# Reordering the start, the hand-over and the end of a one-token attention kernel

## The chip, the cores and the metric

The kernel runs on one core of one Trainium2 chip. The metric is the device time of one execution in microseconds. Every kernel below was timed several times, next to runs of the kernel before on the same chip. PE is the matmul engine, PEld its weight loads, DVE the vector engine, ACT the scalar engine, POOL the GpSimd engine and SP the engine that issues most loads. A letter q after an engine's name means its sequencer. A pair of kernels is compared by the ratio of their times, with its 95% interval in brackets.

## The reference

Two attention layers, A and B, each for one new token and 32 heads of size 128. A looks at all 16384 cached keys of a head, B at the last 4096. The two output rows are joined.

```python
# x: (1,1,512); k_cache, v_cache: (1,32,16384,128); wq: (512,4096); wo: (4096,512); all bf16
q = (x @ wq).reshape(1, 1, 32, 128).transpose(0, 2, 1, 3)
k, v = k_cache, v_cache                                # A
k, v = k_cache[:, :, -4096:], v_cache[:, :, -4096:]    # B
p = softmax(einsum("bhqd,bhkd->bhqk", q, k) * 128**-0.5)
o = einsum("bhqk,bhkd->bhqd", p, v)
out = o.transpose(0, 2, 1, 3).reshape(1, 1, 4096) @ wo
```

The caches are nearly all of the traffic: 80 chunks of 2.1 MB for K, 80 for V, and four weight matrices of 4.2 MB; 352 MB in all.

## The kernel before

SP issues the K chunks and ACT the V chunks, into four buffers each. An A head is two chunks, and in B one chunk holds two heads. DVE works on pairs: the two chunks of an A head, or the two heads of a B chunk. Per pair it multiplies K by a replicated q in place, folds 128 products to 8 with four additions, and reduces them to scores. ACT takes the exponentials (and their row sums, `zp`). PE then multiplies them with V (below: PV) into one PSUM bank per head, two banks in turn, and DVE copies each finished sum to `orow`. In the code, `hg` is the head's number (0 to 31 are A's, 32 to 63 B's), z is the sum of a head's exponentials, ot the output row after scaling with 1/z, transposed, and fin its projection with wo.

```python
# SP: loads
sp.dma_start(xrow[0], xs[0]); sp.dma_start(stage, wqs[0]).then_inc(s_wq, 16); sp.dma_start(xrow[1], xs[1])
sp.wait_ge(s_wq, 16)                      # no K load before wq has landed
for ck, c in enumerate(kchunks):
    if ck == NK:                          # B's wq into the same buffer
        sp.wait_ge(s_qmm, 1); sp.dma_start(stage, wqs[1]).then_inc(s_wq, 16)
    if ck >= NK:
        sp.wait_ge(s_hdone, kchunk_maxhead[ck - NK] + 1)     # DVE is done with the buffer
    sp.dma_start(kbuf[ck % NK], kchunk_src(c)).then_inc(s_kdma[ck % NK], 16)
# ACT: waits for s_wq as well, then V chunks in the same way, as PV frees the buffers
# ... cut ...
# DVE, after each pair:
def head_hooks(hg):
    if hg == 1: qB_copies(0)
    if hg == 3: qB_copies(1)
    if hg - 2 >= 0: orow_copy(hg - 2)     # waits for PV of head hg - 2
    if hg == NHEAD + 1: tail_z(0)         # waits for PE's z matmul: sum of zp, then 1/z
    if hg == NHEAD + 3: tail_ot(0)
# PE, after PV of head hg:
    if hg == NHEAD: tail_pe_z(0); tail_pe_ot(0)     # z; 32 matmuls: orow * (1/z), transposed
    if hg == NHEAD + 4: tail_pe_fin(0)              # 32 matmuls of 512 columns: A's projection
# after head 63: the same for B, one after the other
tail_pe_z(1); tail_pe_ot(1); tail_pe_fin(1)
```

The softmax here doesn't subtract the row's maximum and nothing guards it: scores larger than these inputs give would overflow.

## Time and profile before

The median was 872.11 us (870.71 to 874.21, 4 runs); the profiled execution spans 870.8 us.

| what | value |
|---|---|
| DMA traffic | 353 MB, near 428 GB/s in most of the span |
| DVE busy | 771.6 us, 89% |
| PE busy | 420.7 us, 48% |
| last DVE reduction ends | 850.74 us |
| from there to the end | 20.06 us |

From the page of the kernel before: the busy line (engine, us, share of the span, number of instructions), and the rate of the DMA queues in 40 slices of 21.8 us each.

```profile
PE 420.7 (48%) x5322; PEld 389.5 (45%) x5324; DVE 771.6 (89%) x673; ACT 24.2 (3%) x129; POOL 3.9 (0%) x8
...
GB/s 330 431 426 391 419 415 416 418 426 427 427 427 427 428 423 428 429 427 426 427 425 419 427 428 427 427 427 419 400 428 424 421 420 417 404 404 421 421 294 1
```

The queues are full or nearly so (391 to 431 GB/s, with the DMA engines busy for 90% or more of each slice) from the second slice to the 38th. The next listing, the stretch table of the kernel before, shows where they are not. Its columns are: stretch, its length, busy time and instruction count of PE, PEld, DVE, ACT and POOL, the granted PE clock, DMA share and GB/s.

```profile
12.00:13.00 1.00, 0.00 (x0) 0.00 (x0) 0.00 (x0) 0.00 (x0) 0.00 (x0) 1.00 0.61 255
13.00:14.00 1.00, 0.60 (x4) 0.34 (x4) 0.13 (x1) 0.00 (x0) 0.00 (x0) 1.00 0.00 0
14.00:15.00 1.00, 0.19 (x1) 0.13 (x2) 0.76 (x4) 0.00 (x0) 0.00 (x0) 1.00 0.84 213
...
72.00:74.00 2.00, 2.00 (x21) 1.16 (x19) 2.00 (x5) 0.00 (x0) 0.00 (x0) 1.00 0.77 328
74.00:76.00 2.00, 2.00 (x40) 2.00 (x37) 2.00 (x4) 0.00 (x0) 0.00 (x0) 1.00 0.67 147
```

There is a hole at 12 to 15 us, when wq has landed and nothing else has been issued yet, and a shallower one at 73 to 77 us.

The next listing is the timeline of DVE in the kernel before, around the change from A to B. Its columns are: start, duration, engine, line, operation, result and operands, count, and in brackets the idle time before it and what ended it. L440 is the multiplication that opens a pair.

```profile
665.50 8.76 DVE L440 TENSOR_TENSOR kbuf<-kbuf,qbc 128x8192 bf16<-128x8192 bf16 x2 [0.71 <-DMA kbuf<-in_A_k_cache_dram]
...
684.11 4.47 DVE L440 TENSOR_TENSOR kbuf<-kbuf,qbc 128x4096 bf16<-128x4096 bf16 x2
...
697.19 0.18 DVE L365 COPY zsb<-psum 1x32 f32<-1x32 f32 x1 [3.01 <-PE psum L569]
...
697.96 4.49 DVE L440 TENSOR_TENSOR kbuf<-kbuf,qbc 128x4096 bf16<-128x4096 bf16 x2
...
730.90 0.28 DVE L357 CAST orow<-psum 1x128 bf16<-1x128 f32 x1 [2.98 <-PE psum L623]
731.11 4.47 DVE L440 TENSOR_TENSOR kbuf<-kbuf,qbc 128x4096 bf16<-128x4096 bf16 x2
...
741.11 4.47 DVE L440 TENSOR_TENSOR kbuf<-kbuf,qbc 128x4096 bf16<-128x4096 bf16 x2
```

The last wait for a K load is the one of 0.71 us at 665 us. After 731 us the pairs follow each other at exactly 10.0 us. Between 684 and 731 us two steps are longer, 13.85 and 13.05 us: at 697 DVE had waited 3.01 us for PE's z matmul, and at 731 it had waited 2.98 us for a PV that stood behind the 32 projection matmuls.

The end, from the timeline of the kernel before:

```profile
850.02 0.72 DVE L458 TENSOR_REDUCE s<-kbuf 128x32 bf16<-128x256 bf16 x2
...
851.05 5.95 PE L623 MATMUL psum<-vbuf,e 128*1 128x128 bf16 x64 [4.64 <-ACT e L309]
...
858.05 0.95 PE L581 MATMUL psum<-invz_b,orow 1*128 1x1 bf16 x32 [0.99 <-DVE invz_b L373]
...
859.28 8.67 PE L595 MATMUL psum<-stage,ot_bf 128*1 128x512 bf16 x32 [0.28 <-DVE ot_bf L379]
...
868.00 1.21 DVE L507 CAST out_sb<-psum 1x1024 bf16<-1x1024 f32 x1 [8.77 <-PE psum L595]
```

This is all serial: last reduction, PV of heads 62 and 63, z and 1/z, 32 small matmuls, 32 projection matmuls (8.67 us), copy of the output row, store.

### The profile page before, as it was taken

How to read it: one execution, taken by the hardware profiler on the slowest of the kernel's cores; microseconds unless marked ns; L12 is line 12 of the kernel's file. 1: busy time of each engine (PE TensorE's matmuls, PEld its weight loads, DVE VectorE, ACT ScalarE, POOL GpSimd, SP SyncE). 2: the span in 40 equal slices, each digit the busy share in tenths (PEclk: the TensorE clock that was granted, in tenths of full speed). 3: DMA queues.
4: the chain of work that ended last, by engine and by line, in shares of the span. 5: the costliest groups of instructions: out<-in, count | busy, mean ns of one | idle time of the engine just before them, and what ended most of it. 6: DMA issues, size and time to landing. Idle time of an engine off the chain costs nothing.

```text
span 870.8 us, 11997 instructions
## 1 busy us (share of the span) xinstructions
PE 420.7 (48%) x5322; PEld 389.5 (45%) x5324; DVE 771.6 (89%) x673; ACT 24.2 (3%) x129; POOL 3.9 (0%) x8
## 2 busy tenths in 40 slices
PE   3109644434444444554544444453565447665557
PEld 1006544334444444544544344453565445655544
DVE  0599968798998999999899989988999898999992
ACT  0000000000000000000000000000000000000000
POOL 0000000000000000000000000000000000000000
PEclk9658865667777667677777767676678778678877
DMA  8999999999999999999999999999999999999970
GB/s 330 431 426 391 419 415 416 418 426 427 427 427 427 428 423 428 429 427 426 427 425 419 427 428 427 427 427 419 400 428 424 421 420 417 404 404 421 421 294 1
DMA packets 30330, 353.11 MB, mean 406 GB/s; under 512 B 2627, under 2 KB 2629, under 8 KB 4678
## 3 DMA queue, kind: packets, MB, share of 16 engines
q1 hardware_dynamic: 14630, 176.17, 48.4%
q10 hardware_dynamic: 13568, 167.78, 45.7%
q0 software_dynamic: 2080, 8.39, 2.4%
q8 instruction: 42, 0.69, 0.3%
q14 instruction: 10, 0.08, 0.0%
HBM read 352.32 MB, written 0.00 MB: 405 GB/s over the span
## 4 chain that ended last, share of the span: by engine, by line
DVE 61%; DMA 32%; PE 5%; issue 1%; SPq 1%; DVEq 0%; ACT 0%; ACTq 0%
DMA kbuf<-in_A_k_cache_dram 31%; DVE kbuf L440 28%; DVE kbuf L447 28%; DVE s L458 3%; PE psum L623 3%; PE psum L595 2%; DMA stage<-in_A_wq_dram 1%; DVE orow L357 1%; SPq L274 1%; DVE qbc L341 0%; DVEq L434 0%; DVE out_sb L507 0%; PE psum L581 0%; ACT e L309 0%; ACTq L290 0%
## 5 line engine op out<-in xcount | busy, mean ns | idle before, releaser
L623 PE MATMUL psum<-vbuf,e 128*1 128x128 bf16 x5120 | 382.9, 251 | 389.9 <-ACT e L309 347.3
L623 PEld LDWEIGHTS psum<-vbuf,e 128*1 128x1 bf16 x5120 | 374.0, 99 | 399.3 <-ACT e L309 388.6
L440 DVE TENSOR_TENSOR kbuf<-kbuf,qbc 128x8192 bf16<-128x8192 bf16 (+1 forms) x96 | 351.7, 3702 | 53.6 <-DMA kbuf<-in_A_k_cache_dram 53.5
L447 DVE TENSOR_TENSOR kbuf<-kbuf 128x1024 bf16<-128x1024 bf16 (+4 forms) x384 | 350.0, 980 | 0.0
L458 DVE TENSOR_REDUCE s<-kbuf 128x64 bf16<-128x512 bf16 (+1 forms) x96 | 52.3, 585 | 0.0
L309 ACT ACTIVATE e<-s 128x128 bf16<-128x128 bf16 (+1 forms) x64 | 17.2, 269 | 811.2 <-DVE s L458 771.1
L542 PE MATMUL psum<-stage,xrep 128*128 128x512 bf16 x23 | 7.7, 505 | 41.4 <-DMA stage<-in_B_wq_dram 41.2
L357 DVE CAST orow<-psum 1x128 bf16<-1x128 f32 x64 | 16.1, 269 | 8.6 <-PE psum L623 8.6
L542 PEld LDWEIGHTS psum<-stage,xrep 128*128 128x128 bf16 x24 | 2.9, 125 | 46.2 <-issue 45.1
L595 PE MATMUL psum<-stage,ot_bf 128*1 128x512 bf16 x64 | 16.4, 420 | 0.3 <-DVE ot_bf L379 0.3
L330 DVE CAST xrep<-psum 128x128 bf16<-128x128 f32 x8 | 1.8, 284 | 13.0 <-PE psum L518 13.0
L334 DVE CAST qbc<-psum 128x512 bf16<-128x512 f32 x8 | 4.9, 683 | 9.5 <-PE psum L530 9.5
L309 ACT ACTIVATION_READ_ACCUMULATOR e<-s 128x1 f32 x64 | 11.9, 186 | 0.0
L595 PEld LDWEIGHTS psum<-stage,ot_bf 128*1 128x1 bf16 x64 | 5.8, 92 | 10.1 <-issue 3.2
L530 PE MATMUL psum<-stage,xrep 128*128 128x512 bf16 x32 | 9.4, 465 | 1.0 <-DVE xrep L330 1.0
L507 DVE CAST out_sb<-psum 1x1024 bf16<-1x1024 f32 x1 | 1.2, 1212 | 8.8 <-PE psum L595 8.8
L518 PE MATMUL psum<-ones_row,xrow 1*128 1x128 bf16 x8 | 1.2, 299 | 12.6 <-DMA xrow<-in_B_x_dram 10.5
L530 PEld LDWEIGHTS psum<-stage,xrep 128*128 128x128 bf16 x32 | 3.6, 115 | 6.5 <-issue 3.0
L518 PEld LDWEIGHTS psum<-ones_row,xrow 1*128 1x128 bf16 x8 | 0.7, 124 | 12.9 <-DMA xrow<-in_B_x_dram 10.8
L244 POOL DMA_DIRECT2D stage<-in_B_wo_dram x1 | 1.7, 1682 | 636.2 <-PE psum L595 636.2
L341 DVE CAST qbc<-psum 128x512 bf16<-128x512 f32 x6 | 3.7, 685 | 0.0
L365 DVE COPY zsb<-psum 1x32 f32<-1x32 f32 x2 | 0.3, 174 | 3.0 <-PE psum L569 3.0
(18 smaller groups left out, 13.1 us busy)
## 6 DMA issues: line engine op xcount, KB each, us to landing
kbuf<-in_A_k_cache_dram SPq DMA_DIRECT2D x64, 2048.0 KB, 16.6
vbuf<-in_A_v_cache_dram ACTq DMA_DIRECT2D x64, 2048.0 KB, 17.6
kbuf<-in_B_k_cache_dram SPq DMA_DIRECT2D x16, 2048.0 KB, 23.9
vbuf<-in_B_v_cache_dram ACTq DMA_DIRECT2D x16, 2048.0 KB, 29.8
stage<-in_A_wq_dram SPq DMA_DIRECT2D x1, 4096.0 KB, 12.2
stage<-in_B_wq_dram SPq DMA_DIRECT2D x1, 4096.0 KB, 41.0
stage<-in_A_wo_dram POOLq DMA_DIRECT2D x1, 4096.0 KB, 88.6
stage<-in_B_wo_dram POOLq DMA_DIRECT2D x1, 4096.0 KB, 56.5
```

The costliest lines, as they stand in the source:

```text
L274: sp.dma_start(chunk_dst(kbuf[b], c), kchunk_src(c)).then_inc(s_kdma[b], 16)
L309: act.activation(out=ebuf[b][:, :n_t], in_=sbuf_s[b][:, :n_t], func=mybir.ActivationFunctionType.Exp, scale=SM_SCALE, accum_out=zp[:, hg : ...
L334: ins = dve.tensor_copy(out=qbc[0][:, n * 512 : (n + 1) * 512], in_=bank(n))
L341: ins = dve.tensor_copy(out=qbc[1][:, n * 512 : (n + 1) * 512], in_=bank(2 + n))
L357: dve.tensor_copy(out=orow[0:1, (hg % NHEAD) * DH : (hg % NHEAD + 1) * DH], in_=o_acc(hg % 2),).then_inc(s_orow, 1)
L440: ins = dve.tensor_tensor(out=jb.kview3, in0=jb.kview3, in1=jb.qb, op=mybir.AluOpType.mult)
L447: ins = dve.tensor_tensor(out=jb.kview3[:, :, 0:w], in0=jb.kview3[:, :, 0:w], in1=jb.kview3[:, :, w : 2 * w], op=mybir.AluOpType.add,)
L458: ins = dve.tensor_reduce(out=sbuf_s[jb.b][:, jb.col0 : jb.col0 + jb.rpp], in_=jb.kview3[:, :, 0:RED_W], axis=mybir.AxisListType.X, op=myb ...
L530: ins = pe.matmul(out=bank(n), lhsT=xrep[0][:, c, :], rhs=stage[:, c, n * 512 : (n + 1) * 512], start=(c == 0), stop=(c == 3),)
L542: ins = pe.matmul(out=bank(2 + n), lhsT=xrep[1][:, c, :], rhs=stage[:, c, n * 512 : (n + 1) * 512], start=(c == 0), stop=(c == 3),)
L595: ins4 = pe.matmul(out=psum[0:1, FINBANK * BANK + X * NOUT : FINBANK * BANK + (X + 1) * NOUT], lhsT=ot_bf[:, X * NHEAD + t : X * NHEAD + t ...
L623: last_ins = pe.matmul(out=o_acc(b), lhsT=ebuf[hg % NSE][:, col : col + 1], rhs=vbuf[vb][:, (j0 + j) * DH : (j0 + j + 1) * DH], start=(tdo ...
```

## The change

The intent is (1) to start DVE and the K loads sooner, by loading 512 columns of A's wq first and moving everything that B's q needs to later; (2) to take DVE's waits out of the change from A to B; (3) to do z, the scaling and the projection of B's first 24 heads before the end. The core of the diff, shortened:

```diff
# start, SP
+sp.dma_start(xrow[1], xs[1])
-sp.dma_start(stage, wqs[0]).then_inc(s_wq, 16)
+sp.dma_start(stage[:, :, :512], wqs[0][:, :512]).then_inc(s_wq1, 16)
-sp.wait_ge(s_wq, 16)
 for ck, c in enumerate(kchunks):
+    if ck == 2: sp.dma_start(stage[:, :, 512:], wqs[0][:, 512:]).then_inc(s_wq, 16)
# start, DVE: only q of heads 0..3 is copied first; after head 1:
 if hg == 1:
+    qA_rest_copies(); x_rep_copies(1)
     qB_copies(0)
# start, PE
+x_rep_mms(1) and B's q only after qA_rest_copies
# middle, DVE
-if hg == NHEAD + 1: tail_z(0)
+if hg == NHEAD + 2: tail_z(0)            # one pair later, ahead of orow_copy
# middle, PE
-if hg == NHEAD: tail_pe_z(0); tail_pe_ot(0)
-if hg == NHEAD + 4: tail_pe_fin(0)
+if hg == NHEAD: tail_pe_z(0)
+if hg == NHEAD + 1: tail_pe_ot(0)
+if NHEAD + 4 <= hg < NHEAD + 8: tail_pe_fin(0, (hg - NHEAD - 4) * 8, 8)
# end: B in two segments, heads 32..55 and 56..63
+SEGS = [(0, NHEAD), (NHEAD, NHEAD - 8), (2 * NHEAD - 8, 8)]
+DVE: if hg == 58: tail_z(1);  if hg == 60: tail_ot(1)
+PE:  if hg == 57: tail_pe_z(1);  if hg == 59: tail_pe_ot(1);  if hg == 61: tail_pe_fin(1)
-tail_pe_z(1); tail_pe_ot(1); tail_pe_fin(1)       # 32 heads
+tail_pe_z(2); tail_pe_ot(2); tail_pe_fin(2)       # 8 heads
```

More of the change, by code (lines that the diff above doesn't have):

```diff
@@ L135, in bass_concat_heads__gqa_block_cached__sliding_block_cached__decode_kernel @@
         orow = ctx.enter_context(nc.sbuf_tensor("orow", [1, NHEAD * DH], BF16))
-        zsb = ctx.enter_context(nc.sbuf_tensor("zsb", [1, NHEAD], FP32))
-        invz_f = ctx.enter_context(nc.sbuf_tensor("invz_f", [1, NHEAD], FP32))
-        invz_b = ctx.enter_context(nc.sbuf_tensor("invz_b", [1, NHEAD], BF16))
+        zsb = ctx.enter_context(nc.sbuf_tensor("zsb", [1, 2 * NHEAD], FP32))
+        invz_f = ctx.enter_context(nc.sbuf_tensor("invz_f", [1, 2 * NHEAD], FP32))
+        invz_b = ctx.enter_context(nc.sbuf_tensor("invz_b", [1, 2 * NHEAD], BF16))
         ot_bf = ctx.enter_context(nc.sbuf_tensor("ot_bf", [P, 2 * NHEAD], BF16))
@@ L156, in bass_concat_heads__gqa_block_cached__sliding_block_cached__decode_kernel @@
         s_x = [sem("s_xA"), sem("s_xB")]
+        s_wq1 = sem("s_wq1")
         s_wq = sem("s_wq")
@@ L233, in woA @@
                 def woA():
-                    pool.wait_ge(s_qmm, 3)
+                    pool.wait_ge(s_qmm, 4)
                     pool.dma_start(
@@ L254, in _ @@
                 sp.dma_start(xrow[0][0:1, :], xs[0][0, 0:1, :]).then_inc(s_x[0], 16)
+                sp.dma_start(xrow[1][0:1, :], xs[1][0, 0:1, :]).then_inc(s_x[1], 16)
                 sp.dma_start(
-                    stage_wq_view(), wqs[0][:, :].rearrange("(c p) n -> p c n", p=P)
-                ).then_inc(s_wq, 16)
-                sp.dma_start(xrow[1][0:1, :], xs[1][0, 0:1, :]).then_inc(s_x[1], 16)
+                    stage_wq_view()[:, :, :512],
+                    wqs[0][:, :512].rearrange("(c p) n -> p c n", p=P),
+                ).then_inc(s_wq1, 16)
                 wq_b_issued = False
-                sp.wait_ge(s_wq, 16)
                 for ck, c in enumerate(kchunks):
@@ L263, in _ @@
                     r = ck // NK
+                    if ck == 2:
+                        sp.dma_start(
+                            stage_wq_view()[:, :, 512:],
+                            wqs[0][:, 512:].rearrange("(c p) n -> p c n", p=P),
+                        ).then_inc(s_wq, 16)
                     if ck == NK and not wq_b_issued:
-                        sp.wait_ge(s_qmm, 1)
+                        sp.wait_ge(s_qmm, 2)
                         sp.wait_ge(s_wq, 16)
@@ L325, in dv_inc, with x_rep_copies @@
                     return dv[0]
-                for X in range(2):
+                def x_rep_copies(X):
                     dve.wait_ge(s_xmm, X + 1)
@@ L331, in _, with qA_rest_copies @@
                     ins.then_inc(s_xrep, 1)
+                x_rep_copies(0)
                 dve.wait_ge(s_qmm, 1)
-                for n in range(8):
-                    ins = dve.tensor_copy(out=qbc[0][:, n * 512 : (n + 1) * 512], in_=bank(n))
-                ins.then_inc(s_qcopy, 1)
+                dve.tensor_copy(out=qbc[0][:, 0:512], in_=bank(0)).then_inc(s_qcopy, 1)
+                def qA_rest_copies():
+                    dve.wait_ge(s_qmm, 2)
+                    for n in range(1, 8):
+                        ins = dve.tensor_copy(
+                            out=qbc[0][:, n * 512 : (n + 1) * 512], in_=bank(n)
+                        )
+                    ins.then_inc(s_qcopy, 1)
                 def qB_copies(phase):
                     if phase == 0:
-                        dve.wait_ge(s_qmm, 2)
+                        dve.wait_ge(s_qmm, 3)
                         for n in range(6):
@@ L345, in qB_copies @@
                     else:
-                        dve.wait_ge(s_qmm, 3)
+                        dve.wait_ge(s_qmm, 4)
                         for n in range(6, 8):
@@ L360, in orow_copy, with tail_z @@
                     ).then_inc(s_orow, 1)
-                def tail_z(X):
-                    dve.wait_ge(s_z, X + 1)
+                SEGS = [(0, NHEAD), (NHEAD, NHEAD - 8), (2 * NHEAD - 8, 8)]
+                def tail_z(si):
+                    h0, nh = SEGS[si]
+                    dve.wait_ge(s_z, si + 1)
                     dv_inc(
                         dve.tensor_copy(
-                            out=zsb[0:1, :],
-                            in_=psum[0:1, ZBANK * BANK : ZBANK * BANK + NHEAD],
+                            out=zsb[0:1, h0 : h0 + nh],
+                            in_=psum[0:1, ZBANK * BANK + h0 : ZBANK * BANK + h0 + nh],
                         )
@@ L370, in tail_z, with tail_ot @@
                     dve.wait_ge(s_dv, dv[0])
-                    dv_inc(dve.reciprocal(out=invz_f[0:1, :], in_=zsb[0:1, :]))
+                    dv_inc(dve.reciprocal(out=invz_f[0:1, h0 : h0 + nh], in_=zsb[0:1, h0 : h0 + nh]))
                     dve.wait_ge(s_dv, dv[0])
-                    dve.tensor_copy(out=invz_b[0:1, :], in_=invz_f[0:1, :]).then_inc(
-                        s_zr, 1
-                    )
-                def tail_ot(X):
-                    dve.wait_ge(s_ot, X + 1)
-                    dve.tensor_copy(
-                        out=ot_bf[:, X * NHEAD : (X + 1) * NHEAD],
-                        in_=psum[0:P, OTBANK * BANK : OTBANK * BANK + NHEAD],
+                    dve.tensor_copy(
+                        out=invz_b[0:1, h0 : h0 + nh], in_=invz_f[0:1, h0 : h0 + nh]
+                    ).then_inc(s_zr, 1)
+                def tail_ot(si):
+                    h0, nh = SEGS[si]
+                    dve.wait_ge(s_ot, si + 1)
+                    dve.tensor_copy(
+                        out=ot_bf[:, h0 : h0 + nh],
+                        in_=psum[0:P, OTBANK * BANK + h0 : OTBANK * BANK + h0 + nh],
                     ).then_inc(s_otc, 1)
@@ L429, in job_pre @@
                         dve.wait_ge(s_qcopy, 1)
+                    if hg == 4 and jb.first_of_head:
+                        dve.wait_ge(s_qcopy, 2)
                     if hg == NHEAD and jb.first_of_head:
-                        dve.wait_ge(s_qcopy, 3)
+                        dve.wait_ge(s_qcopy, 4)
                     if hg >= NSE and jb.first_of_head:
@@ L476, in head_hooks @@
                     if hg == 1:
+                        qA_rest_copies()
+                        x_rep_copies(1)
                         qB_copies(0)
@@ L479, in head_hooks @@
                         qB_copies(1)
+                    if hg == NHEAD + 2:
+                        tail_z(0)
                     if hg - 2 >= 0:
                         orow_copy(hg - 2)
-                    if hg == NHEAD + 1:
-                        tail_z(0)
                     if hg == NHEAD + 3:
                         tail_ot(0)
+                    if hg == 2 * NHEAD - 6:
+                        tail_z(1)
+                    if hg == 2 * NHEAD - 4:
+                        tail_ot(1)
                 i = 0
@@ L503, in _ @@
                     orow_copy(hg)
-                tail_z(1)
-                tail_ot(1)
+                tail_z(2)
+                tail_ot(2)
                 dve.wait_ge(s_fin, 2)
@@ L514, in _, with x_rep_mms @@
                 pe.wait_ge(s_ones, 1)
-                for X in range(2):
+                def x_rep_mms(X):
                     pe.wait_ge(s_x[X], 16)
                     for c in range(4):
-                        ins = pe.matmul(
+                        insx = pe.matmul(
                             out=bank(X * 4 + c, 0, P),
@@ L524, in _ @@
                         )
-                    ins.then_inc(s_xmm, 1)
-                pe.wait_ge(s_xrep, 2)
-                pe.wait_ge(s_wq, 16)
+                    insx.then_inc(s_xmm, 1)
+                x_rep_mms(0)
+                pe.wait_ge(s_xrep, 1)
                 for n in range(8):
+                    if n == 0:
+                        pe.wait_ge(s_wq1, 16)
+                    elif n == 1:
+                        pe.wait_ge(s_wq, 16)
                     for c in range(4):
@@ L536, in _ @@
                         )
+                    if n == 0:
+                        ins.then_inc(s_qmm, 1)
                 ins.then_inc(s_qmm, 1)
-                pe.wait_ge(s_qcopy, 1)
+                pe.wait_ge(s_qcopy, 2)
+                x_rep_mms(1)
+                pe.wait_ge(s_xrep, 2)
                 pe.wait_ge(s_wq, 32)
@@ L551, in qB_pass2 @@
                 def qB_pass2():
-                    pe.wait_ge(s_qcopy, 2)
+                    pe.wait_ge(s_qcopy, 3)
                     for n in range(6, 8):
@@ L562, in qB_pass2, with tail_pe_z @@
                     ins2.then_inc(s_qmm, 1)
-                def tail_pe_z(X):
-                    pe.wait_ge(s_exp, NHEAD * (X + 1))
-                    pe.wait_ge(s_qcopy, 3)
-                    if X == 1:
-                        pe.wait_ge(s_otc, 1)
+                SEGS = [(0, NHEAD), (NHEAD, NHEAD - 8), (2 * NHEAD - 8, 8)]
+                def tail_pe_z(si):
+                    h0, nh = SEGS[si]
+                    pe.wait_ge(s_exp, h0 + nh)
+                    pe.wait_ge(s_qcopy, 4)
                     pe.matmul(
-                        out=psum[0:1, ZBANK * BANK : ZBANK * BANK + NHEAD],
+                        out=psum[0:1, ZBANK * BANK + h0 : ZBANK * BANK + h0 + nh],
                         lhsT=ones_col[:, 0:1],
-                        rhs=zp[:, X * NHEAD : (X + 1) * NHEAD],
+                        rhs=zp[:, h0 : h0 + nh],
                         start=True,
@@ L575, in tail_pe_z, with tail_pe_ot @@
                     ).then_inc(s_z, 1)
-                def tail_pe_ot(X):
-                    pe.wait_ge(s_zr, X + 1)
-                    pe.wait_ge(s_orow, NHEAD * (X + 1))
-                    for t in range(NHEAD):
+                def tail_pe_ot(si):
+                    h0, nh = SEGS[si]
+                    pe.wait_ge(s_zr, si + 1)
+                    pe.wait_ge(s_orow, h0 + nh)
+                    for hg in range(h0, h0 + nh):
                         ins3 = pe.matmul(
-                            out=psum[0:P, OTBANK * BANK + t : OTBANK * BANK + t + 1],
-                            lhsT=orow[0:1, t * DH : (t + 1) * DH],
-                            rhs=invz_b[0:1, t : t + 1],
+                            out=psum[0:P, OTBANK * BANK + hg : OTBANK * BANK + hg + 1],
+                            lhsT=orow[0:1, (hg % NHEAD) * DH : (hg % NHEAD + 1) * DH],
+                            rhs=invz_b[0:1, hg : hg + 1],
                             start=True,
@@ L588, in tail_pe_ot, with tail_pe_fin @@
                     ins3.then_inc(s_ot, 1)
-                def tail_pe_fin(X):
-                    pe.wait_ge(s_otc, X + 1)
+                def tail_pe_fin(si, a=0, n=None):
+                    h0, nh = SEGS[si]
+                    X = 0 if h0 < NHEAD else 1
+                    h0, nh = h0 + a, nh if n is None else n
+                    pe.wait_ge(s_otc, si + 1)
                     pe.wait_ge(s_wo, 16 * (X + 1))
                     wo_view = stage_wo_view()
-                    for t in range(NHEAD):
+                    for hg in range(h0, h0 + nh):
+                        h = hg % NHEAD
                         ins4 = pe.matmul(
                             out=psum[0:1, FINBANK * BANK + X * NOUT : FINBANK * BANK + (X + 1) * NOUT],
-                            lhsT=ot_bf[:, X * NHEAD + t : X * NHEAD + t + 1],
-                            rhs=wo_view[:, t, :],
-                            start=(t == 0),
-                            stop=(t == NHEAD - 1),
-                        )
-                    ins4.then_inc(s_fin, 1)
+                            lhsT=ot_bf[:, hg : hg + 1],
+                            rhs=wo_view[:, h, :],
+                            start=(h == 0),
+                            stop=(h == NHEAD - 1),
+                        )
+                    if h0 + nh == NHEAD or h0 + nh == 2 * NHEAD:
+                        ins4.then_inc(s_fin, 1)
                 for hd in heads:
@@ L635, in _ @@
                         tail_pe_z(0)
+                    if hg == NHEAD + 1:
                         tail_pe_ot(0)
-                    if hg == NHEAD + 4:
-                        tail_pe_fin(0)
-                tail_pe_z(1)
-                tail_pe_ot(1)
-                tail_pe_fin(1)
+                    if NHEAD + 4 <= hg < NHEAD + 8:
+                        tail_pe_fin(0, (hg - NHEAD - 4) * 8, 8)
+                    if hg == 2 * NHEAD - 7:
+                        tail_pe_z(1)
+                    if hg == 2 * NHEAD - 5:
+                        tail_pe_ot(1)
+                    if hg == 2 * NHEAD - 3:
+                        tail_pe_fin(1)
+                tail_pe_z(2)
+                tail_pe_ot(2)
+                tail_pe_fin(2)
 _INS = ['A_x', 'A_k_cache', 'A_v_cache', 'A_wq', 'A_wo', 'B_x', 'B_k_cache', 'B_v_cache', 'B_wq', 'B_wo']
```

## The prediction

Two sentences that no trace of this case shows are cut from it where marked. No term of its sum was in them: it is 872.1 - 1.5 - 8.5 = 862 us, as recorded. The two clocks behind its rates can be read in the kernel before: 32 PV matmuls took 1.95 us (61 ns each) at 698.9 us, with a granted clock of 1.00, and the first projections of the end took 0.43 us each from 859.3 to 862.6 us, with a granted clock of 0.50.

> **What bounds the kernel now.** The DMA queues. The stretch table shows 409 to 432 GB/s, a DMA share near 1.0, in nearly every stretch from 16 us to 840 us; 352 MB at about 428 GB/s are 823 of the 870.8 us. [...] DVE, busy 89%, is second: the wait view has it idle 53.5 us for K loads. So work taken off DVE or PE in the middle only lengthens those waits. Time can be won only (a) where the DMA queues are dry and (b) after the last K load.
>
> **(a) Dry queues.** Near 13 us, because K and V are issued only after wq has landed: the stretches between 12 and 18 us lack 2.9 us of traffic. Near 74 us 1.9 us are lacking.
> **(b) The tail.** The traffic stops at 844 us; the last DVE pair runs 841.1 to 850.75. From there 20.05 us are serial: 64 PV matmuls 5.97, z to ot_bf 2.3, 32 projection matmuls 8.7 (0.43 us each for the first 8, then 0.21), copy and store 2.8.
>
> **The start.** wq is cut: 512 columns, then K0 and K1, then the rest. DVE's first multiply moves from 35.8 us to about 14 (estimate: 0.5 + 4.2 MB at 428 GB/s after 2.8 us). I expect nearly all of these 21 us to be lost again: the second head needs K2 and K3, which now share the DMA with V (landing near 42 us, estimate), and after it DVE must copy the rest of qA, rebuild x for B and wait for 24 qB matmuls. Its third head should start near 78 us, as before (77.4). The dry spot at 13 us goes (-2.9 us). The one near 74 us does not: PV of head 0 waits for copies that DVE makes only after its second head, so V buffers come free only near 82 us, when K6 and K7 are about in; 2 to 3.5 us dry. Net: traffic ends 1 to 2 us earlier, K79 with it.
>
> **The middle.** Moving z by one pair and spreading the 32 A projection matmuls over four heads removes DVE stalls of 3.0 and 3.0 us (697, 731 us). DMA was at full rate there: worth about 0.
>
> **The tail.** z, ot and the projection of heads 32 to 55 move ahead, into PE's idle time (53% busy there). The end keeps 8 ot and 8 projection matmuls: 8.7 us become 1.7 to 3.4, ot 0.95 becomes 0.25. The 24 early ones (5 to 6 us) stand directly before the last PV and may delay it by 0.5 us, but leave PE warm: 64 PV matmuls at 61 ns (rate seen at 698 us) are 3.9 instead of 5.97 us. [...] Together 20.05 becomes about 12.
>
> **Sum.** 872.1 - 1.5 - 8.5 = 862 us, range 856 to 867. Faster by over 2% (below 854.7): 0.08; within 2%: 0.91; slower: 0.01.
>
> **What would show it.** First multiply near 14 us but third head near 78; middle rate unchanged, traffic ending near 842; last DVE reduction near 849; then about 12 us.
>
> **What would make it wrong.** A longer dry spot near 80 us; the early B projection delaying the last PV by more than 1 us; or K running ahead of V once DVE stalls less, so that the last V load, not DVE, starts the tail.

## The result, and the profile after

The changed kernel took 858.44 us (median of 11 runs, 856.94 to 860.95), the kernel before 873.1 us (median of its 16 runs by then, 870.68 to 878.45). The ratio is 0.9835, with a 95% interval of 0.9818 to 0.9852. Ratios compare the runs of the two kernels in the same rounds, so they are not quite the ratio of the medians. A gain "by ratio" below is one minus that ratio, times the median of the kernel before in those rounds: here 14.4 us. The range and the class (within 2%) were met.

From the page of the changed kernel, the busy line:

```profile
PE 416.0 (49%) x5324; PEld 384.7 (45%) x5326; DVE 772.5 (90%) x677; ACT 24.1 (3%) x129; POOL 3.9 (0%) x8
```

DVE is busy for 772.5 us, as before: its idle time shrank, its work did not. The stretch table of the changed kernel, where the holes were or were expected:

```profile
12.00:13.00 1.00, 0.00 (x0) 0.00 (x0) 0.00 (x0) 0.00 (x0) 0.00 (x0) 1.00 1.11 475
13.00:14.00 1.00, 0.00 (x0) 0.00 (x0) 0.00 (x0) 0.00 (x0) 0.00 (x0) 1.00 0.74 318
...
80.00:82.00 2.00, 1.34 (x25) 1.34 (x26) 2.00 (x2) 0.40 (x2) 0.00 (x0) 1.00 0.95 401
82.00:84.00 2.00, 2.00 (x39) 2.00 (x37) 2.00 (x1) 0.00 (x0) 0.00 (x0) 1.00 0.95 401
```

The hole at 12 to 15 us is gone, to a dent of 318 GB/s in one microsecond. So is the one at 73 to 77 us: the rate is 393 or more from 72 to 76 us, and 401 or more from there to 90 us.

DVE's timeline of the changed kernel, the same part as before (L460 is now the multiplication):

```profile
681.58 4.47 DVE L460 TENSOR_TENSOR kbuf<-kbuf,qbc 128x4096 bf16<-128x4096 bf16 x2
...
692.15 4.47 DVE L460 TENSOR_TENSOR kbuf<-kbuf,qbc 128x4096 bf16<-128x4096 bf16 x2
...
703.67 0.48 DVE L371 CAST orow<-psum 1x128 bf16<-1x128 f32 x2 [1.17 <-PE psum L619]
...
704.17 4.47 DVE L460 TENSOR_TENSOR kbuf<-kbuf,qbc 128x4096 bf16<-128x4096 bf16 x2
...
784.16 4.47 DVE L460 TENSOR_TENSOR kbuf<-kbuf,qbc 128x4096 bf16<-128x4096 bf16 x2
...
794.87 0.28 DVE L371 CAST orow<-psum 1x128 bf16<-1x128 f32 x1 [0.84 <-PE psum L666]
795.08 4.47 DVE L460 TENSOR_TENSOR kbuf<-kbuf,qbc 128x4096 bf16<-128x4096 bf16 x2
```

B starts 2.5 us earlier, and the steps of 13 us are gone. The two longest steps that are left both have a wait for PE in them: 12.02 us, with 1.17 us for the small matmuls (L619) and the z arithmetic, and 10.92 us, where a sum was copied 0.84 us late because its PV was late. The wait view of the changed kernel (waiter, releaser, us in total, times, longest) gives a reason that the kernel before does not have in its list:

```profile
PE psum L666 <- DMA vbuf<-in_B_v_cache_dram: 30.7, 7, 7.2
```

The end, from the timeline of the changed kernel:

```profile
840.11 5.34 PE L637 MATMUL psum<-stage,ot_bf 128*1 128x512 bf16 x24
...
845.14 0.72 DVE L478 TENSOR_REDUCE s<-kbuf 128x32 bf16<-128x256 bf16 x2
...
846.16 3.73 PE L666 MATMUL psum<-vbuf,e 128*1 128x128 bf16 x64 [0.71 <-ACT e L315]
...
851.37 1.89 PE L637 MATMUL psum<-stage,ot_bf 128*1 128x512 bf16 x8 [0.26 <-DVE ot_bf L397]
853.29 1.21 DVE L533 CAST out_sb<-psum 1x1024 bf16<-1x1024 f32 x1 [1.98 <-PE psum L637]
```

From the last reduction (845.86 us) to the end of the span 10.24 us are left of 20.06. The 24 early projections end at 845.45 us, 0.7 us before the last PV. That PV takes 3.73 instead of 5.95 us, the last projection 1.89 instead of 8.67.

In the two profiles the 14.7 us divide into 2.5 (B starts earlier), 2.4 (from B's start to the last reduction) and 9.8 (from there to the end). The experiments ask what part of the change made each, and why.

### The profile page after: what moved, and what is told of

Same layout as the page of the kernel before. It is cut to its first block, busy times and chain, and to the rows that moved or that the text cites. A ratio compares the mean times of both kernels' runs of the same rounds, so it can differ in the third digit from the quotient of the medians.

```text
span 856.1 us, 12014 instructions
## 1 busy us (share of the span) xinstructions
PE 416.0 (49%) x5324; PEld 384.7 (45%) x5326; DVE 772.5 (90%) x677; ACT 24.1 (3%) x129; POOL 3.9 (0%) x8
## 4 chain that ended last, share of the span: by engine, by line
DVE 49%; DMA 44%; PE 5%; issue 1%; SPq 1%; DVEq 0%; ACT 0%
DMA kbuf<-in_A_k_cache_dram 35%; DVE kbuf L460 22%; DVE kbuf L467 22%; DMA vbuf<-in_B_v_cache_dram 8%; PE psum L666 4%; DVE s L478 3%; PE psum L578 1%; SPq L280 1%; DVE qbc L346 0%; DVE qbc L355 0%; DVE orow L371 0%; PE psum L619 0%; PE psum L637 0%; DVE out_sb L533 0%; DVEq L454 0%
## 5 line engine op out<-in xcount | busy, mean ns | idle before, releaser
L666 PE MATMUL psum<-vbuf,e 128*1 128x128 bf16 x5120 | 378.1, 249 | 378.4 <-ACT e L315 329.8
L666 PEld LDWEIGHTS psum<-vbuf,e 128*1 128x1 bf16 x5120 | 369.2, 98 | 388.7 <-ACT e L315 346.6
L460 DVE TENSOR_TENSOR kbuf<-kbuf,qbc 128x8192 bf16<-128x8192 bf16 (+1 forms) x96 | 351.7, 3703 | 58.2 <-DMA kbuf<-in_A_k_cache_dram 57.2
L619 PE MATMUL psum<-invz_b,orow 1*128 1x1 bf16 x64 | 2.1, 160 | 6.3 <-DVE invz_b L390 6.3
L619 PEld LDWEIGHTS psum<-invz_b,orow 1*128 1x128 bf16 x64 | 1.9, 95 | 6.7 <-DVE invz_b L390 6.6
## 6 DMA issues: line engine op xcount, KB each, us to landing
vbuf<-in_B_v_cache_dram ACTq DMA_DIRECT2D x16, 2048.0 KB, 31.1
```

What stands on the lines that cost most here:

```text
L460: ins = dve.tensor_tensor(out=jb.kview3, in0=jb.kview3, in1=jb.qb, op=mybir.AluOpType.mult)
L619: ins3 = pe.matmul(out=psum[0:P, OTBANK * BANK + hg : OTBANK * BANK + hg + 1], lhsT=orow[0:1, (hg % NHEAD) * DH : (hg % NHEAD + 1) * DH], ...
L666: last_ins = pe.matmul(out=o_acc(b), lhsT=ebuf[hg % NSE][:, col : col + 1], rhs=vbuf[vb][:, (j0 + j) * DH : (j0 + j + 1) * DH], start=(tdo ...
```

## The experiments

Two readings compete. The one of the prediction: DMA bounds everything up to the end, so time is won only where its queues ran dry, and after the last load. The rival: from about 684 us on DVE waits for no K load, so DVE bounds the B heads, and the stalls taken out of the middle are real time.

### One part of the change at a time

Each of the three kernels is the kernel before with one group of the hunks above; the other two groups are left as they were. All three ran on one chip, next to the same runs of the kernel before (median 872.78 us).

`start_only`:

```diff
+the hunks marked "start" (split wq, K0 and K1 ahead of its rest, B's q later)
 tail_z, tail_pe_ot and tail_pe_fin as in the kernel before
```

> Only the new order of the start; the tail and the middle as in the kernel before. Theory (time is won where the DMA queues were dry, and at the tail): last DVE reduction and end both 2 to 4 us earlier than in the kernel before, ratio 0.995 to 0.998. Rival (the 21 us by which DVE starts earlier are worth something in themselves): more than 5 us earlier. Rival 2 (DVE stalls in the middle gave all of the 4.9 us by which the last reduction came earlier): 0 us, ratio 1.000.

Measured: 870.71 us, ratio 0.9966 (0.9942 to 0.9989), or 3.0 us by ratio. The first multiplication was at the same 15 us as in the changed kernel, 21 us earlier than in the kernel before, B's first one at 681.29 us instead of 684.11, and the last reduction at 848.66 us instead of 850.74. Of 21 us, 3 reached the end.

`middle_only`:

```diff
-if hg == NHEAD + 1: tail_z(0)
+if hg == NHEAD + 2: tail_z(0)
-if hg == NHEAD: tail_pe_z(0); tail_pe_ot(0)
+if hg == NHEAD: tail_pe_z(0)
+if hg == NHEAD + 1: tail_pe_ot(0)
-if hg == NHEAD + 4: tail_pe_fin(0)
+if NHEAD + 4 <= hg < NHEAD + 8: tail_pe_fin(0, (hg - NHEAD - 4) * 8, 8)
 start and end as in the kernel before
```

> Only the middle of the change: z of the first 32 heads one pair later on DVE, their projection spread over four heads; start and end as in the kernel before. Theory as predicted (DMA was at full rate there): 0 to 1 us, ratio 0.999 to 1.001. Rival (from about 684 us on DVE waits for no K load in either trace, so DVE is the bound there and its stalls of 6 us, less the new ones of 2 us, are real time): 2 to 4 us earlier, ratio 0.995 to 0.998.

Measured: 871.1 us, ratio 0.9971 (0.9945 to 0.9997), or 2.5 us by ratio: the rival's number, though the upper end of the interval still touches the prediction's 0 to 1 us. The trace and `before_no_woB` below decide. DVE's timeline of this kernel, two pairs at the change from A to B and two near the end:

```profile
695.10 4.47 DVE L444 TENSOR_TENSOR kbuf<-kbuf,qbc 128x4096 bf16<-128x4096 bf16 x2
...
707.13 4.47 DVE L444 TENSOR_TENSOR kbuf<-kbuf,qbc 128x4096 bf16<-128x4096 bf16 x2
...
817.89 4.47 DVE L444 TENSOR_TENSOR kbuf<-kbuf,qbc 128x4096 bf16<-128x4096 bf16 x2
...
828.28 4.49 DVE L444 TENSOR_TENSOR kbuf<-kbuf,qbc 128x4096 bf16<-128x4096 bf16 x2 [0.25 <-issue]
```

From its first B multiplication to its last reduction it takes 162.9 us; the kernel before takes 166.6. The steps of 13.85 and 13.05 us have become 12.03 and 10.0. Steps above 10.0 turn up later, as the 10.39 us before 828.28, and the wait view of this kernel has PV waiting for B's V loads seven times, 31.1 us in all.

`tail_only`:

```diff
+SEGS = [(0, NHEAD), (NHEAD, NHEAD - 8), (2 * NHEAD - 8, 8)], with z, ot and projection of
+heads 32..55 after heads 57, 59 and 61
 start and middle as in the kernel before
```

> Only the early z, ot and projection of heads 32 to 55; start and middle as in the kernel before. Theory: from the last DVE reduction to the end 10 to 10.5 us instead of 20, and the reduction itself within 1 us of the kernel before (it gets about 1 us of z work on DVE earlier), so 9 to 10 us in all, ratio 0.988 to 0.990. Rival: the end moves by less, 6 to 7 us, because the 24 early projections only come cheap when the rest of the change is there.

Measured: 865.16 us, ratio 0.9897 (0.9873 to 0.9921), or 9.0 us by ratio. From the last reduction to the end it took 10.63 us in the profile. The reduction itself came 1.9 us later than in the kernel before's profile, where 1 us was expected at most. 1.1 us of that was there already at B's first multiplication (685.18), before this kernel differs in anything that runs, and some 0.7 us are the z work and the copy of `ot_bf` that now stand between DVE's last pairs.

The three parts add up: 3.0 + 2.5 + 9.0 = 14.5 us, against 14.4 of the whole. As each is uncertain by about 2 us, so close a match is in part luck.

### What the start is worth, and why

`no_gap` is the kernel before without one line:

```diff
 wq_b_issued = False
-sp.wait_ge(s_wq, 16)
 for ck, c in enumerate(kchunks):
```

> The kernel before with one line less: the K queue no longer waits for wq before it issues the first four K loads, so these stand right behind wq in the same queue. wq is not split and V still waits for wq. Theory (the start is worth what the dry spot near 13 us cost): the first B multiply near 681 instead of 684 us and the end 2 to 3 us earlier, ratio 0.996 to 0.998, as in the run with the new start alone (0.9966). Rival (the split of wq and the DVE start at 15 us are what pays): 0 to 1 us, ratio 0.999 or more.

Measured: 870.28 us, ratio 0.9957 (0.994 to 0.9974), or 3.8 us by ratio. As far as the intervals tell, the removed line is worth as much as the whole new start (3.0 us, on another chip). DVE's timeline of this kernel, the multiplications (L439) of the first and third head:

```profile
29.77 8.76 DVE L439 TENSOR_TENSOR kbuf<-kbuf,qbc 128x8192 bf16<-128x8192 bf16 x2
...
74.43 8.75 DVE L439 TENSOR_TENSOR kbuf<-kbuf,qbc 128x8192 bf16<-128x8192 bf16 x2
```

DVE starts at 29.77 us, far later than with the new start (14.88), and its third head at 74.43 us is still the earlier one (75.70 in the changed kernel, 77.35 before). So the early start of DVE at 15 us is not what paid. The first multiplication comes 6.0 us sooner than in the kernel before (35.80), with the K loads right behind wq. The hole near 74 us goes too: `simple` (below), which has the same start, moved 414 GB/s or more in every stretch of 2 us from 72 to 84 us, where the kernel before fell to 147. B's first multiplication came at 680.4 to 682.1 us in eight of the nine profiles of kernels with the new or the one-line start and four buffers each for K and V (the ninth, 686.5 us, is of the kernel `no_woB` below and fell on its slowest run), and at 684.1 to 685.2 us in the four with the old start.

`simple` puts that one-line start under the middle and the end of the change:

```diff
 start of the kernel before
-sp.wait_ge(s_wq, 16)
 middle and end of the changed kernel
```

> Middle and tail of the change, but the start of the kernel before with only the K queue's wait for wq removed (wq whole, DVE starts near 30 us instead of 15). Theory (of the start only the filled dry spot near 13 us counts, not the early DVE): 0.982 to 0.985 of the kernel before, within 1.5 us of the changed kernel. Rival (the early DVE start adds to it once the tail is shorter): 2 us or more slower than the changed kernel, 0.986 or more.

`after_again` is the changed kernel itself, beside it on the same chip:

```diff
 (the changed kernel, no edit)
```

> The changed kernel itself once more, as the measure for the two runs beside it on the same chip. Every theory: 0.9835 of the kernel before, within the interval of 0.982 to 0.985.

Measured: `after_again` 859.67 us, ratio 0.9837 (0.9819 to 0.9856); `simple` 858.14 us, ratio 0.9828 (0.9813 to 0.9843). The split of wq, its extra semaphore and the moved q copies can be left out, at no loss that the runs show.

### What bounds the B heads

Both kernels were run without the 4.2 MB load of B's wo, which falls into the B heads. Their B output is wrong, as A's wo is used twice.

```diff
 woA()
-woB()
-pe.wait_ge(s_wo, 16 * (X + 1))
+pe.wait_ge(s_wo, 16)
```

> The kernel before without the 4.2 MB load of B's wo; the second half of the output is wrong on purpose (A's wo is used in its place). If DMA bounds the B heads, as the prediction had it, some 9.8 us less traffic bring the end 5 to 9.8 us earlier, ratio 0.989 to 0.994. If DVE bounds them from 684 us on (16 pairs at a pitch of 10.0 us and 7 us of stalls, no K wait), the end moves by less than 1 us, ratio 0.999 to 1.001, while the traffic ends earlier.

> The same taken away from the changed kernel, wrong on purpose in the same way. If with the shorter stalls DMA has become the bound there (PV waits for V seven times, 31 us in all, and hold DVE up by some 2 us), the last DVE reduction comes about 2 us earlier and the end with it: about 0.981 of the kernel before. If DMA bounds the B heads fully: 5 us or more, 0.978 or less. If DVE alone: no change, 0.9835.

`before_no_woB`: 873.35 us, ratio 0.9994 (0.9976 to 1.0013). No gain shows: by the interval it is 2.1 us at most, where 5 to 9.8 us were expected of a kernel bound by DMA. Its stretch table and DVE timeline:

```profile
832.00:834.00 2.00, 2.00 (x22) 2.00 (x20) 2.00 (x2) 0.00 (x0) 0.00 (x0) 0.50 0.01 4
```

```profile
841.23 4.47 DVE L439 TENSOR_TENSOR kbuf<-kbuf,qbc 128x4096 bf16<-128x4096 bf16 x2
```

The traffic was over by 832 us, where that of the kernel before lasted to 844, and the last DVE pair still started at 841.23 us (841.07 before). In the B heads of the kernel before, DVE with its two stalls for PE was the bound, not DMA.

`no_woB`, the same taken from the changed kernel: 857.49 us, ratio 0.9811 (0.979 to 0.9832), where the changed kernel had 0.9835 and 0.9837. That is about 2 us, as expected of a kernel in which DMA has become a part of the bound, but the intervals overlap, so the size is not shown. Its profile fell on its slowest run (861.61 us), so its absolute times are left out. From the first B multiplication to the last reduction it takes 162.4 us, against 164.3 and 165.5 in the changed kernel's two profiles, and its wait view has no PV that waits for V. But `simple` and `better`, with the load of wo, come to 163.2 and 162.7 us.

`four_acc` attacks the waits for a late PV from DVE's side: four PSUM banks for the PV sums, so that DVE copies a sum four heads later and need not wait for a late PV.

```diff
-def o_acc(b): return psum[0:1, b * BANK : b * BANK + DH]
+def o_acc(b): b = (0, 1, 6, 7)[b]; return psum[0:1, b * BANK : b * BANK + DH]
-if hg - 2 >= 0: orow_copy(hg - 2)
+if hg - 4 >= 0: orow_copy(hg - 4)        # A's tail_ot and tail_pe_ot two heads later
-if hg >= 2: pe.wait_ge(s_orow, hg - 1)
+if hg >= 4: pe.wait_ge(s_orow, hg - 3)
```

> The changed kernel with four PSUM banks for the PV sums instead of two, so DVE copies a head's sum four heads later and does not wait for a PV that waits for V. Theory (the 4.3 us by which the 16 B pairs exceed 160 us are such waits): first B multiply to last reduction 161 to 162 us instead of 164.3 unless K loads become the wait, the end 1.5 to 3 us earlier than the changed kernel, 0.980 to 0.982 of the kernel before. Rival (DMA sets the pace and K waits replace these waits): no change, 0.9835.

Measured: 859.06 us (4 runs), ratio 0.9832 (0.9805 to 0.9858): no gain that shows, and 165.3 us for the B heads instead of the 161 to 162 expected, as the rival had it. DVE's timeline of this kernel, two pairs in a row:

```profile
786.05 4.49 DVE L461 TENSOR_TENSOR kbuf<-kbuf,qbc 128x4096 bf16<-128x4096 bf16 x2 [3.04 <-DMA kbuf<-in_B_k_cache_dram]
...
796.95 4.49 DVE L461 TENSOR_TENSOR kbuf<-kbuf,qbc 128x4096 bf16<-128x4096 bf16 x2 [0.81 <-DMA kbuf<-in_B_k_cache_dram]
```

DVE's waits for PE are gone from the B heads, and it waits 3.04 and 0.81 us for K loads. It is not shown that the one came in place of the other, for `after_again`, the changed kernel with its two banks, has such a wait too:

```profile
785.55 4.49 DVE L460 TENSOR_TENSOR kbuf<-kbuf,qbc 128x4096 bf16<-128x4096 bf16 x2 [2.93 <-DMA kbuf<-in_B_k_cache_dram]
```

So what DMA costs DVE in the B heads varies from profile to profile. Counting K waits, and waits for a PV that had waited for V, it is 0.84 and 2.93 us in the two profiles of the changed kernel, 2.74 in `cold` (below) and 3.85 here; with the start of the kernel before or the one-line start it is 0.51 in `middle_only`, 0.35 in `simple` and 0 in `better`. Whether the new start is the reason for the larger ones was not tested.

### What the place of the early projection is worth

`cold` moves z, ot and projection of heads 32 to 55 one pair earlier, so that PE is idle before the last PV:

```diff
-DVE: hg == 58: tail_z(1);  hg == 60: tail_ot(1)
+DVE: hg == 56: tail_z(1);  hg == 58: tail_ot(1)
-PE:  hg == 57: z;  hg == 59: ot;  hg == 61: fin
+PE:  hg == 55: z;  hg == 57: ot;  hg == 59: fin
```

> The changed kernel with the z, ot and projection of heads 32 to 55 each one DVE pair earlier, so that PE is idle before the last 64 PV matmuls; no instruction is added or removed. Theory (the early projection standing directly before them keeps the PE clock up): last PV 5.5 to 6 us instead of 3.73, the last 8 projections 2.5 to 3.4 instead of 1.89, in all 3 to 4 us slower than the changed kernel. Rival (the place does not matter, only that 24 of 32 heads are done early): within 1 us of the changed kernel.

Measured: 860.37 us, ratio 0.9849 (0.9823 to 0.9875), within the noise of the changed kernel (0.9835); 3 to 4 us more were expected. The timeline of its end:

```profile
846.16 5.08 PE L666 MATMUL psum<-vbuf,e 128*1 128x128 bf16 x64 [4.12 <-DVE orow L371]
...
852.72 1.89 PE L637 MATMUL psum<-stage,ot_bf 128*1 128x512 bf16 x8 [0.26 <-DVE ot_bf L397]
```

The last PV took 5.08 instead of 3.73 us, so the place is worth 1.35 us to that PV. The last 8 projections took the same 1.89 us, so the rest of the expected 3 to 4 us did not come. On the other hand the place has a cost, which the profile of `after_again` shows:

```profile
836.36 6.58 PE L666 MATMUL psum<-vbuf,e 128*1 128x128 bf16 x64 [2.23 <-DVE orow L371]
...
842.77 5.34 PE L637 MATMUL psum<-stage,ot_bf 128*1 128x512 bf16 x24
...
847.95 3.74 PE L666 MATMUL psum<-vbuf,e 128*1 128x128 bf16 x64
```

Here the PV of heads 60 and 61 ran at the slow clock (granted 0.50 from 836 to 842 us, 6.58 us in all), the 24 projections behind it lasted to about 848 us, and the last PV, which stands behind them, started at 847.95 us: 2.0 us after the last reduction (845.95) instead of 0.3. From the last reduction to the end it took 11.95 us, not 10.24. In the changed kernel's first profile the same PV ran at a granted clock of 1.00 (3.73 us). So the end of this kernel differs by 1.7 us between the two profiles with the clock that PE has one pair before.

### Attempts at something better

`four_acc_k5v3` has the four banks, and five K and three V buffers instead of four and four:

```diff
-NK = 4; NV = 4
+NK = 5; NV = 3
```

> Four PSUM banks for the PV sums as in the run before, and five K buffers with three V buffers instead of four and four (the same memory). Theory (in the B heads DMA and DVE are both close to the bound, and K and V share the queues; with V behind K, the K waits of 3.0 and 0.8 us go and DVE comes near 160 us for its 16 pairs, while the last V load lands before DVE is done): last DVE reduction 2 to 4 us earlier than in the changed kernel, end 2 to 4 us earlier, 0.979 to 0.981 of the kernel before. Rival (three V buffers starve the queues or the PV): slower than the changed kernel, 0.985 or more.

Measured: 869.0 us, ratio 0.9951 (0.9936 to 0.9966), 10 us slower by ratio than the changed kernel beside it. Its waits (the kernel before and the changed kernel have no line of PV waiting for A's V loads), and the start of its second B pair on DVE:

```profile
ACT e L316 <- PE psum L667: 541.1, 29, 23.1
PE psum L667 <- DMA vbuf<-in_A_v_cache_dram: 285.8, 58, 8.1
```

```profile
689.02 4.49 DVE L461 TENSOR_TENSOR kbuf<-kbuf,qbc 128x4096 bf16<-128x4096 bf16 x2 [19.71 <-ACT e L316]
```

With three V buffers and two chunks to an A head, PV waits for V in nearly every A head, ACT issues no exponentials behind it, and DVE at last waits 19.71 us for ACT. K had run ahead, as intended (B's first multiplication was at 658.88 us), and all of it was given back at the change from A to B.

In the profile of `simple` the 24 projections held the last PV up as well: it started at 846.03 us, 1.6 us after the last reduction.

`better` is `simple` with two repairs:

```diff
 z, ot of heads 32..55 one pair earlier, as in the run called cold
-PE: tail_pe_fin(1) in one piece
+PE: hg == 59: tail_pe_fin(1, 0, 12);  hg == 61: tail_pe_fin(1, 12, 12)
+DVE, before the last orow copies: A's half of out_sb is copied
-out_sb <- psum, 1x1024, at the end
+out_sb <- psum, 1x512, at the end
```

> The one-line start, the middle and the tail of the change, and two repairs of the tail: z, ot and projection of heads 32 to 55 one DVE pair earlier, with 12 of the 24 projections after head 59 and 12 after head 61 (in the run with the one-line start all 24 stood in front of the last PV and held it up by 1.3 us); and A's half of the output row is copied while DVE waits for the last PV. Theory (traffic end and serial tail add up): last PV at most 0.4 us after the last reduction and still at the fast clock (3.7 us for 64), final copy 0.6 to 0.7 instead of 1.21 us; 1 to 2 us faster than the run with the one-line start, 0.980 to 0.982 of the kernel before. Rival (V loads decide when the last PVs run): no change, 0.983.

Measured: 857.78 us, ratio 0.9811 (0.9794 to 0.9828), the lowest ratio of a correct kernel here. The timeline of its end:

```profile
844.87 5.36 PE L642 MATMUL psum<-vbuf,e 128*1 128x128 bf16 x64 [2.73 <-DVE orow L356]
...
853.63 0.68 DVE L519 CAST out_sb<-psum 1x512 bf16<-1x512 f32 x1 [1.98 <-PE psum L613]
```

The PV starts 0.3 us after the last reduction, and the final copy is 0.68 us. But one expectation failed: PE was idle for 2.73 us before the PV, and the PV took 5.36 us. Against `simple` (0.9828, another chip) and the changed kernel (0.9837) the intervals overlap, so it is clearly faster than the kernel before, and that it beats the changed kernel or `simple` is not shown.

## Why the prediction was right, and where it was not

- **The sum.** 862 us with a range of 856 to 867 was predicted, 858.44 measured. The range held. A gain of 10.0 us was forecast and 14.4 came; by the parts, 1.5 us of the difference lie in the start, 2.5 in the middle and 0.5 in the tail, each uncertain by about 2 us. The middle term had the wrong mechanism, and the range held because it was 11 us wide and that term small.
- **"Work taken off DVE or PE in the middle only lengthens those waits"; "DMA was at full rate there: worth about 0".** This step was wrong. Alone, the middle was worth 2.5 us, and its B heads were 3.7 us shorter in the profile. Full DMA queues did not mean that DMA was the bound: the waits of 53.5 us for K all lie before 666 us, the traffic ran ahead of DVE, and with 4.2 MB less of it the traffic was over by 832 us instead of 844 while the time stayed (0.9994). The prediction spread over the whole span a wait that belonged to the A heads alone. The stalls of 6 us were not worth 6 us either, since z and the small matmuls kept a wait of their own (12.03 us for one pair) and since PV then began to wait for V (31.1 us in `middle_only`).
- **The start: early DVE lost again, the hole at 13 us won.** Right, and shown by `no_gap`, which issues the K loads right behind wq without the early start. The third head started at 75.7 us, where 78 was predicted. The term was too small, 1 to 2 us against 3.0, which fits the next point.
- **"The one near 74 us does not [go]", 2 to 3.5 us dry.** Wrong in size: there was no dry spot. K2 and K3 landed by 39.5 us rather than 42, PV of head 0 ended at 79.3 us rather than 82, and K6 and K7 were still loading. In `simple`, with the start of `no_gap`, this hole went as well, without the split. K then loads beside V: from 23.5 us, when V's first loads are issued, 4.2 MB of K alone would need 9.8 us at 428 GB/s (an estimate from the rate of the trace); it took 16, at 419 GB/s for all loads together.
- **The tail: 20.05 becomes "about 12".** 10.24 us in one profile of the changed kernel, 11.95 in the other; 9.0 us by ratio as a part alone. The last PV at the fast clock was right (3.73 us, 3.9 predicted). The delay by the early projection was sized at 0.5 us; it was 0 in one profile and about 1.7 in the other. In the five other profiles with the projection in this place the last PV started 0.2 to 1.3 us later than the 0.3 us after the reduction at which it starts otherwise.
- **The clock.** In these profiles the granted clock near the end is 0.50 for 3.4 us (859.2 to 862.6 in the kernel before, 845.6 to 849.0 in `cold` and `better`) or for 6.8 to 6.9 us (848.9 to 855.7 in the kernel before, 835.5 to 842.4 in `after_again`), with 1.00 before and after. The same 64 PV matmuls cost 3.73, 5.08, 5.36, 5.95 or 6.58 us, of which 0, 2.9, 3.4, 4.7 and 6.0 us were at 0.50. What takes the clock down is not shown. In the kernel before, 2.3 us passed between the last PV and the projection, 0.95 us of them busy with the small matmuls, and the projection began at 0.50; in the changed kernel 1.5 us passed, and the clock stayed at 1.00.
- **"K running ahead of V once DVE stalls less".** Named as a risk, and seen: PV waits for V seven times, 30.7 us, a line that the kernel before's list does not have. In this profile DVE lost 0.84 us by it, and the larger losses elsewhere were waits for K. It did not decide the end, where the traffic stopped 5 us before the last PV.

What stays open: how much of the 3.0 us of the start the early DVE might add or cost (the one-line start was 0.8 us better by ratio, on another chip, with overlapping intervals), and whether `better` beats the changed kernel by more than chance.

## What to carry to other kernels

In this kernel full DMA queues were the bound only where DVE's waits ended in a load (53.5 us in the A heads of the kernel before): read the wait list stage by stage, and test it by taking a load away (here 4.2 MB less gave 0.9994). Before splitting a load to start an engine sooner, look for the hole in the queue rate; one wait fewer at the issuing engine may be the whole gain (3.8 us in `no_gap`, by ratio). Work moved out of the serial end was paid nearly in full here (9.0 us by ratio, for an end that was 9.4 us shorter in the profile of `tail_only`), but look at what it stands in front of. And profile the same kernel twice before you put down a wait of 3 us to an edit (the changed kernel lost 0.84 us to a PV behind V in one profile, 2.93 us to a K load in the other).
